# Three edits to a planned instruction order, a product over all 128 rows and a narrower last piece

## The chip, the cores and the metric

The kernel runs on one core of one Trainium2 chip. The metric is the device time in microseconds (us); lower is better.

## The reference, cut to what matters

A linear attention with decay (retention) is followed by a layer normalisation, a feed-forward block and a residual sum.

```python
# q, k, v: 4 x 8 x 768 x 64 float32
for t in range(S):
    state = gamma * state + einsum('bhd,bhe->bhde', k[:, :, t], v[:, :, t])
    y[:, :, t] = scale * einsum('bhd,bhde->bhe', q[:, :, t], state)
x = y.transpose(0, 2, 1, 3).reshape(4, 768, 512)
xn = (x - mean(x)) / sqrt(var(x) + 1e-6) * g_ln
out = x + relu(xn @ w_ch1) @ w_ch2          # 512 -> 2048 -> 512
```

## The kernel before

The 3072 rows are 24 tiles of 128. Tiles 0 to 3 are the first chunks of the four batches and need no state; tiles 4 to 23 are the later chunks. A tile passes through these steps, under the names that the profile shows:

- `tp<-idn,k`, `tp<-idn,qsb`: k and q transposed on TensorE (tiles 0 to 7; from tile 4 on k is called `ksb`).
- `pa<-trq,trk`: the scores. `asb`: the scores times the decay mask, on VectorE ("mask n" below).
- `py<-v,asb`: the masked scores times v ("py n").
- Statistics and `xn` on VectorE; `tp<-idn,xn`: x transposed on TensorE ("x n"); `xnt`: its copy.
- `mm<-xnt,w`: a product of the first layer. 16 matmuls, 0.89 us, are one product of a one-tile group. w1 arrives in four quarters, and product m(n, quarter i) needs the i-th.
- `mm<-zeros`: filler. Until 20 us the planner puts products on zeros into TensorE's planned gaps. They count as busy.
- `tp<-w,h`: a product of the second layer.
- `vg`: v times decay, on GpSimd; `pd<-vg,k`: the state product, which needs it.

The order of the instructions on every engine is decided by a planner inside the program. It puts tasks on engines one at a time, by the earliest *planned* start and then by rank. Durations and load landings are numbers in the code, so a planned number changes the order, and how many fillers there are, and nothing else:

```python
def add(self, eng, ns, rank, emit, after=(), takes=None, uses=(), load=0, lat=0, at=0, follows=()): ...
# ... in order():
            if t["load"]:
                dma_free = max(dma_free, t["end"]) + t["load"]
                t["seen"] = dma_free + self.load_lat + t["lat"]     # planned landing
```

The parts that the change touches:

```python
ones = const.tile([1, P], FP32, name="ones")
grow = const.tile([1, DM], FP32, name="grow")
...
small = a(DVE, 1200, -100, c_small)                    # constants, on VectorE
nc.tensor.matmul(p, lhsT=ones, rhs=grow, ...)          # spreads g over 128 rows
...
loaded[kind, j] = a(POOL, ns, rank, emit, (), takes, uses, dma,
    1500 if kind in "qkv" and j > 7 else 0 if kind in "qkv" else 600, follows=follows)   # "lat"
...
am = a(DVE, 1230, r + 1, e_am, [pat, maskd], ("asb", t), [("pa", t)])      # mask n
xnn = a(DVE, 750, r + 3, e_xn, [bn, gl], ("xn", t), [("py", t)])           # xn n
pdt = a(PE, 230, r - 1 if cc == 0 else r + 2.2, e_pd, [vgt, loaded["k", j]] + ...)
...
for t, cols in [(t, slice(0, DM)) for t in range(NT - 1)] + [              # second layer
        (NT - 1, slice(i * DM // 2, (i + 1) * DM // 2)) for i in range(2)]:
```

## Time and profile before

| what | before |
|---|---|
| time | 217.70 us, median of 3 runs (217.66 to 217.73) |
| the profiled execution | 217.94 us, span 216.2 us, mean clock 0.992 |
| TensorE busy | 207.7 us, 96% |
| VectorE, ScalarE, GpSimd busy | 56%, 39%, 41% |
| first matmul of the last tile | 208.93 us |
| from there to the end of the span | 7.24 us |

Read this by stages, not by the 96%. The profiled execution is 0.24 us above the median, and it is the one that all traces below are compared with. TensorE takes its instructions in order, so a wait costs most where work that is ready stands behind it: in this trace py 3 was ready with its mask at 22.68 and ran at 24.03, behind the wait for `ksb`.

### The profile page before, as it was taken

What the parts mean: (1) busy time and instruction counts of PE and PEld (TensorE: products, weight loads), DVE (VectorE), ACT (ScalarE), POOL (GpSimd) and SP (SyncE); (2) the same over time, 40 slices, a digit from 0 to 9 for tenths busy, and PEclk for the clock granted to TensorE, in tenths of its full rate; (3) what the DMA queues carried; (4) which work ended last, traced back from release to release, by engine and by line L of the source; (5) the groups of instructions that cost most, each with busy time, mean ns of one, the idle gap of its engine ahead of it and who ended that gap; (6) DMA issues with size and microseconds to landing.
All of it is one profiled execution on the core that took longest, in us unless ns stands there. A gap on an engine that the chain in (4) does not pass through costs nothing.

```text
span 216.2 us, 4571 instructions
## 1 busy us (share of the span) xinstructions
PE 207.7 (96%) x1887; PEld 131.8 (61%) x1906; DVE 120.1 (56%) x229; ACT 84.9 (39%) x157; POOL 89.6 (41%) x105
## 2 busy tenths in 40 slices
PE   7898799999999999999999999999999999999993
PEld 7687799996656577566657544554544444444452
DVE  6686677991127987999899855861511100111121
ACT  5456466865222325333316533563442334332000
POOL 8997697969953269863596100000000000000000
PEclk9889999999999999999999999999999999999999
DMA  7999999999999999999999993111121001110212
GB/s 143 178 180 179 180 156 196 206 162 146 134 183 184 176 208 132 142 184 167 193 149 172 127 229 87 50 24 36 40 73 49 13 36 52 49 49 0 100 51 95
DMA packets 106694, 26.51 MB, mean 123 GB/s; under 512 B 99377, under 2 KB 103729, under 8 KB 106674
## 3 DMA queue, kind: packets, MB, share of 16 engines
q0 software_dynamic: 75984, 13.24, 82.0%
q1 hardware_dynamic: 29506, 12.59, 30.1%
q10 hardware_dynamic: 1184, 0.39, 0.7%
q8 instruction: 15, 0.25, 0.4%
q14 instruction: 5, 0.04, 0.1%
HBM read 27.27 MB, written 6.29 MB: 155 GB/s over the span
## 4 chain that ended last, share of the span: by engine, by line
PE 87%; DMA 8%; POOL 2%; issue 1%; DVE 0%; POOLq 0%
PE tp L617 38%; PE mm L580 37%; DMA ksb<-in_k_dram 4%; DMA w<-in_moe_w_ch_dram 3%; PE pa L434 3%; PE py L457 2%; PE pd L503 2%; PE py L453 2%; PE tp L533 1%; PE tp L395 0%; POOL k L337 0%; POOL state L267 0%; PE tp L402 0%; POOL vg L490 0%; POOL qsb L337 0%
## 5 line engine op out<-in xcount | busy, mean ns | idle before, releaser
L580 PE MATMUL mm<-xnt,w 128*128 128x128 bf16 (+2 forms) x768 | 93.7, 273 | 0.5 <-ACT xnt L184 0.5
L617 PE MATMUL tp<-w,h 128*128 128x512 bf16 (+1 forms) x381 | 86.5, 370 | 1.2 <-issue 0.3
L593 ACT ACTIVATE h<-mm 128x512 bf16<-128x512 f32 x91 | 54.4, 598 | 78.8 <-PE mm L580 78.7
L580 PEld LDWEIGHTS <-w 128*128 128x128 bf16 x768 | 58.3, 98 | 24.7 <-issue 0.5
L617 PEld LDWEIGHTS <-h 128*128 128x128 bf16 x400 | 38.0, 98 | 38.4
L625 DVE SCALAR_TENSOR_TENSOR osb<-tp,rstd,x_all 128x512 f32<-128x512 f32 (+1 forms) x25 | 18.2, 728 | 69.0 <-PE tp L617 68.9
L441 DVE TENSOR_TENSOR asb<-pa,mask 128x1024 bf16<-128x1024 f32 x24 | 29.3, 1219 | 7.3 <-PE pa L434 7.0
L471 DVE BATCH_NORM_STATS2 bns<-py 128x6 f32<-128x512 f32 x24 | 16.7, 697 | 10.7 <-PE py L457 10.2
L490 POOL TENSOR_TENSOR vg<-vsb,vsc 128x512 bf16<-128x512 bf16 x16 | 17.2, 1076 | 10.1 <-DMA vsb<-in_v_dram 4.8
L477 ACT CAST x_all<-py 128x512 bf16<-128x512 f32 x24 | 14.0, 582 | 16.7 <-DVE xn L466 15.6
L337 POOL DMA_DIRECT2D vsb<-in_v_dram x20 | 18.1, 909 | 2.1 <-PE py L457 2.1
L337 POOL DMA_DIRECT2D qk<-in_k_dram x16 | 14.7, 920 | 10.1 <-DMA tr<-qk 8.1
L466 DVE SCALAR_TENSOR_TENSOR xn<-py,mv,gb 128x512 bf16<-128x512 f32 x24 | 18.0, 751 | 0.9
L517 DVE TENSOR_TENSOR state<-pd,gch 64x256 bf16<-64x256 f32 x40 | 16.7, 418 | 0.8 <-PE pd L503 0.5
L337 POOL DMA_DIRECT2D qk<-in_q_dram x16 | 14.3, 894 | 2.0 <-DMA w<-in_moe_w_ch_dram 1.4
L641 PE MATMUL mm<-zeros 128*128 128x128 bf16 x84 | 9.3, 277 | 1.0 <-DVE zeros L217 1.0
L424 DVE TENSOR_TENSOR trq<-tr,qsc 128x512 bf16<-128x512 bf16 x16 | 8.4, 527 | 0.2
L641 PEld LDWEIGHTS <-zeros 128*128 128x128 bf16 x84 | 7.5, 129 | 1.3 <-DVE zeros L217 1.0
L457 PEld LDWEIGHTS <-asb 128*128 128x128 bf16 x192 | 8.1, 99 | 0.1
L457 PE MATMUL py<-vsb,asb 128*128 128x64 bf16 x160 | 7.9, 193 | 0.0
L453 PE MATMUL py<-state,trq 128*128 128x128 bf16 x80 | 7.7, 219 | 0.0
L453 PEld LDWEIGHTS <-trq 128*128 128x128 bf16 x80 | 5.8, 98 | 2.3
(64 smaller groups left out, 116.2 us busy)
## 6 DMA issues: line engine op xcount, KB each, us to landing
out_dram<-osb SPq DMA_DIRECT2D x23, 256.0 KB, 2.0
w<-in_moe_w_ch_dram POOLq DMA_DIRECT2D x8, 512.0 KB, 9.7
vsb<-in_v_dram POOLq DMA_DIRECT2D x20, 128.0 KB, 8.8
qk<-in_k_dram POOLq DMA_DIRECT2D x16, 128.0 KB, 8.4
qk<-in_q_dram POOLq DMA_DIRECT2D x16, 128.0 KB, 8.6
qsb<-in_q_dram POOLq DMA_DIRECT2D x7, 128.0 KB, 7.8
ksb<-in_k_dram POOLq DMA_DIRECT2D x4, 128.0 KB, 9.1
k<-in_k_dram POOLq DMA_DIRECT2D x3, 128.0 KB, 7.1
```

The source lines that it names most:

```text
L337: nc.gpsimd.dma_start(out=tile_of(kind, j), in_=src)
L441: nc.vector.tensor_tensor(out=take("asb", t, [P, NPAIR, 2, P], BF16).rearrange("p i a t -> p a i t"), in0=held["pa", t], in1=mask.rearrang ...
L453: nc.tensor.matmul(py[:, 2 * i:2 * i + 2, :], lhsT=held["trq", t][:, i, :], rhs=held["pb", t][:, i, :], start=(mi == 0), stop=False)
L457: nc.tensor.matmul(py[:, h, :], lhsT=held["asb", t][:, h // 2, h % 2, :], rhs=tile_of("v", t)[:, h, :], start=(mi == 0), stop=(mi == n - 1))
L466: nc.vector.scalar_tensor_tensor(out=take("xn", t, [P, DM], BF16), in0=held["py", t].rearrange("p h d -> p (h d)"), scalar=mv[:, t, 0:1], ...
L471: nc.vector.bn_stats(out=bns[:, t, :], in_=held["py", t].rearrange("p h d -> p (h d)"))
L490: e.tensor_tensor(out=take("vg", j, [P, H, D], BF16), in0=tile_of("v", j), in1=vsc[:, cc, :].unsqueeze(2).to_broadcast([P, H, D]), op=ALU. ...
L580: nc.tensor.matmul(p[:, j, :], lhsT=w1[:, ko, (ho + j) * P:(ho + j + 1) * P], rhs=held["xnt", hb][:, h0:h0 + n, ko, :], start=(ko == 0), s ...
L593: nc.scalar.activation(out=dst, in_=src, func=AF.Relu)
L617: nc.tensor.matmul(held[key], lhsT=held["h1", hb][:, ho, i * P:(i + 1) * P], rhs=w2[:, ho, cols], start=(ho == 0), stop=(ho == HO - 1))
L625: nc.vector.scalar_tensor_tensor(out=take("osb", key, [P, w], FP32), in0=held[key], scalar=rstd[:, t:t + 1], in1=x_all[:, t, cols], op0=AL ...
L641: nc.tensor.matmul(held["mm", "warm"][:, 0:P], lhsT=zeros, rhs=zeros, start=True, stop=True)
```

## The change

Five parts:

1. g is multiplied over all 128 rows (zeros below the first), meant to keep TensorE's clock up; this costs a memset.
2. Mask n of tiles 1 to 3 is planned behind xn of tile n-1.
3. q, k and v of tiles 2 to 7 are *planned* to land 0.8 us later, and those of tile 1 0.6 us later; no load is moved by this alone.
4. The first state product is planned at 20 us or later.
5. The last tile's two column halves become 384 and 128 columns.

```diff
-    ones = const.tile([1, P], FP32, name="ones")
-    grow = const.tile([1, DM], FP32, name="grow")
+    ones = const.tile([P, P], FP32, name="ones")
+    grow = const.tile([P, DM], FP32, name="grow")
...
+        nc.vector.memset(grow, 0.0)
...
-    small = a(DVE, 1200, -100, c_small)
+    small = a(DVE, 1450, -100, c_small)
...      (the load of g now fills row 0 and waits for small)
-   1500 if kind in "qkv" and j > 7 else 0 if kind in "qkv" else 600,
+   1500 if kind in "qkv" and j > 7 else 800 if kind in "qkv" and j > 1 else 600,
...
-        am = a(DVE, 1230, r + 1, e_am, [pat, maskd], ("asb", t), [("pa", t)])
+        am = a(DVE, 1230, r + 1, e_am, [pat, maskd] + ([xnn] if 0 < t < 4 else []), ("asb", t), [("pa", t)])
...
-   [("vg", j), where["k", j]] + ([("pd", b)] if cc else []))
+   [("vg", j), where["k", j]] + ([("pd", b)] if cc else []), at=0 if cc or b else 20000)
...
-            (NT - 1, slice(i * DM // 2, (i + 1) * DM // 2)) for i in range(2)]:
+            (NT - 1, slice(0, DM - P)), (NT - 1, slice(DM - P, DM))]:
```

At the first use of `am` for a tile, `xnn` is still that of the tile before, which is what part 2 uses.

More of the change, by code (lines that the diff above doesn't have):

```diff
@@ L292 @@
     grd = a(SP, 390, -150, lambda eng: nc.sync.dma_start(
-        out=grow, in_=moe_g_ln.rearrange("(o n) -> o n", o=1)), load=10)
+        out=grow[0:1, :], in_=moe_g_ln.rearrange("(o n) -> o n", o=1)), [small], load=10)
     gbm = a(PE, 1000, 2, c_gb, [grd, small2], ("mm", "g"), at=7600)
```

## The prediction

> **What bounds the kernel now.** I began with the busy shares over the span on the page, then cut the span into windows.
>
> ```profile
> PE   7898799999999999999999999999999999999993
> ...
> PEclk9889999999999999999999999999999999999999
> ...
> DMA  7999999999999999999999993111121001110212
> ```
>
> Each digit is a fortieth of the span, 5.4 us. TensorE is full from the fifth or sixth digit to the last but one; before that it is not, and there the DMA engines are full. So there are three stages: a head that lives on loads, a body of pure TensorE work, and a tail after the last matmul.
>
> ```profile
> core 0: us, PE busy (x) PEld busy (x) DVE busy (x) ACT busy (x) POOL busy (x), PEclk, DMA share, GB/s
> ...
> 9.40:12.80 3.40, 3.40 (x42) 3.00 (x40) 2.69 (x6) 1.42 (x7) 2.97 (x5) 0.53 1.99 171
> ...
> 20.00:24.30 4.30, 2.59 (x47) 2.06 (x45) 2.19 (x3) 2.17 (x5) 2.24 (x4) 1.00 1.95 176
> 24.30:212.40 188.10, 186.78 (x1610) 114.12 (x1625) 103.00 (x182) 72.62 (x132) 69.80 (x76) 1.00 1.09 118
> 212.40:216.20 3.80, 0.19 (x2) 0.00 (x0) 0.48 (x1) 0.00 (x0) 0.00 (x0) 1.00 0.18 61
> ```
>
> In the body, 24.3 to 212.4, PE is busy 186.8 of 188.1 us. The few steps there between two 512-column matmuls that are 0.43 us and not 0.22 are lost records, not waits: the group of the second product has 381 records of the 400 that its weight loads count. So the time is: end of the body = (real matmul work, which the change leaves alone) + (TensorE time in the head that did no real work), then a tail of 3.8 us. The change can gain only by doing more real work before about 24 us, or by shortening the tail. The window 20.0 to 24.3 is the worst: 1.7 us of 4.3 are empty. Who is waited for there:
>
> ```profile
> PE tp L395 <- DMA ksb<-in_k_dram: 0.8, 1, 0.8
> PE mm L580 <- ACT xnt L184: 0.5, 1, 0.5
> PE tp L395 <- DMA k<-in_k_dram: 0.5, 1, 0.5
> PE tp L533 <- DVE xn L466: 0.4, 1, 0.4
> ```
>
> The timeline puts three of the four there, and the k load at 7.5:
>
> ```profile
> 16.71 1.95 PE L580 MATMUL mm<-xnt,w 128*128 128x128 bf16 x32
> ...
> 18.50 0.40 PE L457 MATMUL py<-v,asb 128*128 128x64 bf16 x8
> ...
> 20.69 0.40 PE L533 MATMUL tp<-idn,xn 128*128 128x128 bf16 x4 [0.38 <-DVE xn L466]
> ...
> 21.96 1.05 PE L580 MATMUL mm<-xnt,w 128*128 128x128 bf16 x16 [0.55 <-ACT xnt L184]
> ...
> 23.80 0.40 PE L395 MATMUL tp<-idn,ksb 128*128 128x128 bf16 x4 [0.78 <-DMA ksb<-in_k_dram]
> ```
>
> TensorE runs in order. The transpose of tile 4's k, at 23.80, waits for a load that lands at 23.75, while tile 3's py (mask ready at 22.68) and a 16-matmul product of w1's third quarter (landed 22.39) stand behind it. That is the wait to remove.
>
> **What the Trainium skill says.** "TensorE: Matmul & The Clock Gate", Part 1, says the clock halves or doubles by windows of 3413 ns. The trace agrees: the granted clock is 0.5 for one 3.41 us record, 9.21 to 12.62, and matmuls step by 107 ns there against 56 before and after. The page gives idleness as the cause; here PE was busy 2.95 of the 3.5 us before, but 0.5 us of it was the one-row product for g. Whether one row counts as idle the page does not say; the change bets on it. Its rules section says a product over few rows takes the time of one over 128, so all rows should cost nothing against today's 1.12 us. "VectorE: DVE Perf Modes", on zero memsets, gives one cycle per element whatever the type; 128 f32 took 0.17 us and one took 0.06 here, so the new 512-wide memset is, as an estimate, 0.06 + 511 x 0.11/127 = 0.5 us. "DMA: Bandwidth & Descriptors", Anatomy, gives about 2.0 us fixed per DMA; the stores here land in 2.0 us at 256 KB and 1.7 at 128 KB, so a smaller last store saves little.
>
> **The change part by part.** I compared the built order of both kernels, engine by engine.
>
> *Memset of 128x512 on VectorE, all rows of ones:* +0.5 us in the constants. VectorE ends them at 4.77 and is then idle 0.47 until q lands (5.24): at most 0.1 us late, and see below for why that is lost anyway. The small load of g now waits for the memset (about 0.5 us later); its product starts near 8 us.
>
> *Masking of tiles 1 to 3 behind the x of the tile ahead:* VectorE's order of these is already mask, statistics, x, mask. The new edge pins it. 0.
>
> *Tile 0's scores before tile 1's k transpose:* takes it from behind the k wait. Scores 0 started at 7.79 though trq was ready at 7.31: 0.35 us sooner.
>
> *g over 128 rows:* if the clock stays full, the chain from 9.2 to 12.5 (q1 transpose, py0, scores 1, x0 transpose, each 0.53 to 0.63 instead of 0.40) is about 0.3 to 0.7 us sooner.
>
> *First state product put off:* the state update, two instructions of 0.42 us, leaves its place between trq2 (ends 15.89) and mask 2 (starts 16.68): mask 2 about 0.45 us sooner.
>
> These could make tile 2 more than 1 us earlier, but all of that meets one load: w1's second quarter, issued at 7.51, lands at 17.31, and py2 stands behind its product. It starts at 17.60 now, so at most 0.25 us of it survives: py2 at 18.25.
>
> *Loads of tiles 2 to 7 planned later:* this is the part that pays. From py2, with durations of the trace (16 matmuls 0.89, a transpose set 0.22, py 0.23, scores 0.33): k3 18.5, product 18.7 to 19.6, q3 and first state product to 20.1, x2 transpose 20.45 (0.24 sooner), scores 3 at 20.8. State update now comes before mask 3: mask 3 ends 22.75, as before. Then two products in place of one, 21.7 to 23.5, py3 to 23.75, k4 as it lands (23.8 to 24.0), product to 24.9, q4, product to 26.05, x3 transpose. It was at 27.17 with the same work done: 1.1 us ahead.
>
> *What is given back:* the order of GpSimd's queue changes too. Tile 7's k load is now issued ahead of tile 4's vg. GpSimd comes free at 26.03; issue 0.94, then vg 1.06: vg4 ends at 28.0 instead of 27.11. Its product stands right behind scores 4, which TensorE now reaches at 27.2 and leaves at 27.5: a new wait of 0.5 us. From 28.05 the lead is about 0.6 us. A little slack upstream changes nothing, as vg4 hangs on issues and landings alone.
>
> *Behind that:* VectorE has no idle time from 36.75 to 49.7, with slack of 0.2 us at tile 7's scores. The new order answers: one 0.69 us relu of that stretch goes to ScalarE and one product moves ahead of tile 7's scores. I keep the 0.6. The later loads have 4 us and more to spare from landing to use, and the last groups have the old order.
>
> *Tail:*
>
> ```profile
> 210.94 0.48 DVE L625 SCALAR_TENSOR_TENSOR osb<-tp,rstd,x_all 128x256 f32<-128x256 f32 x1 [1.05 <-PE tp L617]
> 212.63 0.48 DVE L625 SCALAR_TENSOR_TENSOR osb<-tp,rstd,x_all 128x256 f32<-128x256 f32 x1 [1.21 <-PE tp L617]
> 213.15 0.36 ACTq L632 DMA_DIRECT2D out_dram<-osb  x1
> ```
>
> The halves of 256 become 384 and 128 columns. Matmuls: 32 x 0.109 = 3.49 us before; 16 x 0.163 (between 0.109 and 0.216) + 16 x 0.056 = 3.50 after. The last VectorE step: 512 columns take 0.75 and 256 take 0.48, so 128 take 0.35: -0.13. The last store has 64 KB for 128: about -0.1 by the slope above, less if the larger store, now issued only 0.6 us ahead, is in its way. -0.15 in all.
>
> Sum: -0.6 - 0.15 = -0.75, from 217.7 to 216.95; I say 216.9.
>
> **The rivals.** (a) *The loads bind, and nothing moves:* DMA is 90% full and more until 130 us, and the change moves no byte. For it: w1's landings at 17.3 and 22.4. Against it: between those TensorE has real work ready and stands still for order alone. Then only the tail is left: 217.5. (b) *vg4 does not hold:* the v4 data are there at 24.9; if GpSimd's issues come sooner, the whole 1.1 us and the tail come through: 216.4. (c) *VectorE takes over at 37 to 49 us:* a lead cannot pass an engine without idle time. For it: no gap there. Against: the moved relu, and products that need no VectorE to fill in. It would leave 0 to 0.3: 217.3. (d) *The clock:* if the half-speed record moves to 12.6 to 16.0, where real products begin, 16 matmuls cost 1.7 and not 0.9 us: py1 and x1 late, up to +0.5 after the meeting point at 17.3: 217.5.
>
> **Range and chances.** The terms run from -0.15 to -1.3, the middle near -0.75; I widen for landings that shift by some tenths: 216.2 to 217.5. Two per cent is 4.4 us, more than all empty TensorE time of the head after 12 us, so within 2% is all but sure.
>
> **What would show it.** Right: PE's wait for ksb at tile 4's k near 0; the x3 transpose near 26.05; a new wait of PE's state product for vg of some 0.5 us near 27.5; no granted clock of 0.5 at 9.2 to 12.6, with py2 still near 18.25; the dense body ending at about 211.8; the last VectorE step 0.35. Wrong: w1's second quarter landing elsewhere than 17.3, PE waits for VectorE between 37 and 50, or new gaps of PE in the body.

## The result, and the profile after

| | runs, us | median |
|---|---|---|
| before, in the same rounds | 217.66 to 217.82 | 217.71 |
| changed | 217.65, 216.83, 216.84, 216.83 | 216.84 |

The ratio is 0.9968, with a 95% interval of 0.9945 to 0.9992. A ratio here is the mean time of one kernel's runs over that of the other's of the same rounds, so it is not quite the ratio of the medians. The medians differ by 0.87 us: faster. The three shorter runs have spans of 215.0 us; **the profiled execution is the slowest of the four**, 217.65 with a span of 215.8, which matters below.

The busy shares in forty slices, after:

```profile
PE   7888899999999999999999999999999999999993
PEclk9999999999999999999999999999999999999999
DMA  7999999999999999999999993111121011110212
```

The second and third digits of the clock were 8 and are 9: no half-speed record in the head. (One begins at 214.86, after the last matmul.) The rest has the old shape, so the gain has to be sought in single waits. The same windows as before:

```profile
core 0: us, PE busy (x) PEld busy (x) DVE busy (x) ACT busy (x) POOL busy (x), PEclk, DMA share, GB/s
...
9.40:12.80 3.40, 2.73 (x49) 2.20 (x46) 3.07 (x5) 1.60 (x5) 2.89 (x5) 1.00 1.97 173
20.00:24.30 4.30, 2.82 (x47) 2.32 (x45) 2.62 (x5) 2.00 (x4) 1.96 (x3) 1.00 1.96 177
24.30:212.40 188.10, 186.76 (x1606) 113.24 (x1620) 103.44 (x181) 73.90 (x133) 69.90 (x77) 1.00 1.07 118
212.40:216.20 3.80, 0.04 (x1) 0.00 (x0) 0.35 (x1) 0.00 (x0) 0.00 (x0) 0.82 0.21 69
```

In 9.4 to 12.8 the clock is 1.00 and not 0.53. In 20.0 to 24.3, where the gain was to come from, TensorE is busy 2.82 us and not 2.59: little. Who it waits for:

```profile
PE mm L581 <- DMA w<-in_moe_w_ch_dram: 0.9, 1, 0.9
...
PE tp L534 <- DVE xn L467: 0.6, 1, 0.6
PE mm L581 <- ACT xnt L184: 0.4, 1, 0.4
```

The wait for `ksb`, 0.8 us before, is gone, as planned, but one for a quarter of w1 stands in its place. The timeline places it:

```profile
16.19 2.16 PE L581 MATMUL mm<-xnt,w 128*128 128x128 bf16 x32 
18.18 0.40 PE L458 MATMUL py<-v,asb 128*128 128x64 bf16 x8 
...
20.38 0.40 PE L534 MATMUL tp<-idn,xn 128*128 128x128 bf16 x4 [0.23 <-ACT h L594]
...
21.48 1.05 PE L581 MATMUL mm<-xnt,w 128*128 128x128 bf16 x16 [0.38 <-ACT xnt L184]
23.41 1.07 PE L581 MATMUL mm<-xnt,w 128*128 128x128 bf16 x16 [0.88 <-DMA w<-in_moe_w_ch_dram]
...
24.54 0.39 PE L396 MATMUL tp<-idn,ksb 128*128 128x128 bf16 x4 
```

The second of the two products that now stand ahead of tile 4's k needs w1's third quarter. It landed at 22.39 before and at 23.36 here. The tail:

```profile
211.64 0.62 DVE L626 SCALAR_TENSOR_TENSOR osb<-tp,rstd,x_all 128x384 f32<-128x384 f32 x1 [1.90 <-PE tp L618]
212.48 0.35 DVE L626 SCALAR_TENSOR_TENSOR osb<-tp,rstd,x_all 128x128 f32<-128x128 f32 x1 [0.22 <-PE tp L618]
212.86 0.36 ACTq L633 DMA_DIRECT2D out_dram<-osb  x1
```

The last VectorE step is 0.35 and not 0.48 us. From the last tile's first matmul (208.78) to the end of the span it is 7.04 us, before 7.24. So in this execution the head gave 208.93 - 208.78 = 0.15 and the tail 0.20. In the three shorter runs, if their tail is the same, the last tile starts at 215.0 - 7.04 = 207.96, about 0.8 us earlier than here. What differs between executions of one program is the first question for the experiments.

### The profile page after: what moved, and what is told of

It is laid out like the page before. It is cut to its first block, busy times and chain, and to the rows that moved or that the text cites. A ratio compares the mean times of both kernels' runs of the same rounds, so it can differ in the third digit from the quotient of the medians.

```text
span 215.8 us, 4578 instructions
## 1 busy us (share of the span) xinstructions
PE 206.9 (96%) x1892; PEld 130.7 (61%) x1910; DVE 120.3 (56%) x229; ACT 86.2 (40%) x158; POOL 89.7 (42%) x105
## 4 chain that ended last, share of the span: by engine, by line
PE 86%; DMA 9%; POOL 1%; DVE 1%; issue 1%; POOLq 0%
PE tp L618 38%; PE mm L581 37%; DMA w<-in_moe_w_ch_dram 9%; PE pa L435 3%; PE pd L504 2%; PE py L458 2%; PE py L454 2%; DVE asb L442 1%; PE tp L534 1%; DVE trq L425 0%; POOL k L338 0%; PE tp L403 0%; PE tp L396 0%; POOL qsb L338 0%; POOL v L338 0%
## 5 line engine op out<-in xcount | busy, mean ns | idle before, releaser
L618 PE MATMUL tp<-w,h 128*128 128x512 bf16 (+2 forms) x382 | 86.4, 370 | 1.1 <-issue 0.2
L594 ACT ACTIVATE h<-mm 128x512 bf16<-128x512 f32 x92 | 55.0, 598 | 75.9 <-PE mm L581 75.6
L618 PEld LDWEIGHTS <-h 128*128 128x128 bf16 x400 | 37.4, 98 | 39.1
L626 DVE SCALAR_TENSOR_TENSOR osb<-tp,rstd,x_all 128x512 f32<-128x512 f32 (+2 forms) x25 | 18.2, 729 | 68.3 <-PE tp L618 68.2
L425 DVE TENSOR_TENSOR trq<-tr,qsc 128x512 bf16<-128x512 bf16 x16 | 9.5, 591 | 0.3
L642 PE MATMUL mm<-zeros 128*128 128x128 bf16 x88 | 8.6, 260 | 1.0 <-DVE zeros L217 1.0
```

The lines of the kernel that those rows point to most:

```text
L594: nc.scalar.activation(out=dst, in_=src, func=AF.Relu)
L618: nc.tensor.matmul(held[key], lhsT=held["h1", hb][:, ho, i * P:(i + 1) * P], rhs=w2[:, ho, cols], start=(ho == 0), stop=(ho == HO - 1))
L626: nc.vector.scalar_tensor_tensor(out=take("osb", key, [P, w], FP32), in0=held[key], scalar=rstd[:, t:t + 1], in1=x_all[:, t, cols], op0=AL ...
```

## The experiments

**My theory:** the planned landings make the gain in the head, and it depends on w1's third quarter landing by 22.4; the split makes the tail; parts 1, 2 and 4 are worth nothing. **The rivals:** the late quarter is a lasting effect of the new order; the clock makes the gain; the other edges matter.

All twelve kernels were correct, with five rounds each. The first four ran on one chip, beside 11 runs of before with a median of 217.71; the other eight on a second chip, beside 11 or 12 with a median of 217.92 or 217.89. I compare kernels within a chip. "w1 third" is that quarter's landing in the profiled execution.

| kernel | median (range), us | ratio [95%] | w1 third |
|---|---|---|---|
| *first chip* | | | |
| changed kernel again | 217.0 (216.75 to 217.27) | 0.9964 [0.9951, 0.9977] | 23.16 |
| without the later landings | 217.53 (217.43 to 218.23) | 0.9997 [0.9985, 1.0009] | 22.18 |
| g over one row | 217.06 (216.71 to 219.51) | 0.9987 [0.9954, 1.0019] | 22.42 |
| tile 7's k held back (missed) | 216.98 (216.63 to 218.12) | 0.9971 [0.9953, 0.9989] | 22.15 |
| *second chip* | | | |
| tile 7's k behind vg 4 | 217.06 (216.9 to 217.24) | 0.9958 [0.9941, 0.9975] | 22.30 |
| w1 third planned later | 216.92 (216.81 to 217.17) | 0.9955 [0.9935, 0.9974] | 22.48 |
| both of these | **216.72** (216.59 to 217.47) | 0.9947 [0.9928, 0.9965] | 22.20 |
| last tile in halves | 217.22 (217.2 to 217.28) | 0.9965 [0.9948, 0.9981] | 22.21 |
| without the mask edge | 217.98 (217.44 to 218.48) | 0.9998 [0.9977, 1.0019] | 22.44 |
| state product not put off | 216.94 (216.85 to 217.22) | 0.9953 [0.9937, 0.9969] | 22.34 |
| before + later landings only | 217.48 (217.01 to 217.92) | 0.9978 [0.9958, 0.9997] | 22.20 |
| four loads planned as seen | 217.37 (217.17 to 217.51) | 0.9971 [0.9955, 0.9986] | 22.33 |

### The changed kernel again

No edit.

> The changed kernel unaltered, for more of its times and a second trace. The profiled execution of it took 217.65 us and not 216.83 like the other three, and in its trace w1's third quarter landed at 23.36 where the kernel before had it at 22.39; the product of tile 0 with it waited 0.9 us. Theory: two kinds of execution, by that landing. A trace of a 216.8 us execution has the landing near 22.4, PE's wait for w near 0, and a wait of some 0.5 us of tile 4's state product for vg near 27.5. Rival: the landing is always near 23.4 and the short executions gain elsewhere; then the trace of a short one still shows the 0.9 us wait.

The gain repeats (0.71 us between the medians; whether this is another chip than that of the first result is not on record), and so does the late quarter: 23.16, with a wait for it.

```profile
PE mm L581 <- DMA w<-in_moe_w_ch_dram: 1.0, 1, 1.0
```

So it is not a single accident. But it is not in every execution either. The kernels below that have the same order up to that point saw it at 22.1 to 22.5, as the kernel before did. In 14 traces it was late twice, both times in the unaltered changed kernel, and the load is issued at the same place in the queue in all of them. Two of two against none of twelve might look like the changed kernel's own. Against that, three of its four first runs were 0.8 us faster than the one that was profiled; and the kernel with the halves at the end, whose head has the same order, saw 22.21. What moves the landing by 1 us is not shown. The traces do hold a lead. A load's semaphore counts sixteen steps. In the 12 early traces fifteen steps of the third quarter are in by 21.28 to 21.62 and the last comes at 22.15 to 22.48; in the two late ones the fifteenth comes at 22.32 and 22.01, the sixteenth at 23.36 and 23.16. In all 14 traces one 16 KB transfer of queue q8, which the profile calls "instruction", runs for 0.89 to 0.95 us from about 14; then the second quarter's fifteenth step is in by 16.20 to 16.55 and its sixteenth 0.6 to 1.2 us later. So the landing near 17.3 at which everything meets is itself one straggler of sixteen. A second such transfer starts at 20.9 to 21.7 (22.5 without the mask edge), while the third quarter arrives. This suggests that a fetch of instructions holds up one of the load's steps; but the packets don't name the DMA engine, so it is likely and not shown.

How much does the late quarter cost? The kernel with the halves has the same head and the early quarter. Against it the profiled changed execution is 0.88 us behind at 26.5, but only 0.32 from 29.65 on, since it has no wait for vg 4; a wait of 0.18 for VectorE's `trq` at 67.93, which two kernels with an early quarter also have, makes most of the rest of the 0.63 at the last tile (208.78 against 208.15). So the late quarter costs some 0.3 us, and not all of the 0.8 between the first result's runs. Where the rest lies stays open.

### Without the later landings

```diff
-   800 if kind in "qkv" and j > 1 else 600
+   0 if kind in "qkv" else 600
```

> The changed kernel with the planned landing of tiles 2 to 7 put back to the old value. In the built order k4's transpose is again ahead of py3 and of tile 0's product with w1's third quarter, and tile 7's k load is again behind tile 4's vg; the rest of the change stays. Theory (the later loads are the part that pays, 0.6 us): 217.4 to 217.6, with a wait of some 0.8 us for ksb at 23.8. Rival (loads bind anyway; clock, masks and tail make the gain): 216.8 to 216.9.

The old wait comes back:

```profile
PE tp L396 <- DMA ksb<-in_k_dram: 0.7, 1, 0.7
```

The medians leave 217.71 - 217.53 = 0.18 us of gain, which is the tail's 0.20. (The means, with one run of 218.23 among these, leave 0.07.) The edit takes back tile 1's 0.6 too: running the planner, without the chip, shows that tile 1's number alone only puts tile 0's scores ahead of tile 1's k transpose, and tiles 2 to 7 make the rest of the new order. This part carries the head's gain.

### g over one row

```diff
-    ones = const.tile([P, P], FP32, name="ones")
+    ones = const.tile([1, P], FP32, name="ones")      # grow likewise; no memset, no edge from small
```

> The changed kernel with g's product over one row again and no memset of 128x512; every engine's order else is the same. Theory (all of the head meets at the landing of w1's second quarter at 17.3): time within 0.1 us of the changed kernel, 216.8, with or without a half-speed record at 9 to 13 us. Rival (the clock makes the gain): 217.2 or more, with a granted clock of 0.5 in the windows 9.4 to 12.8.

The bet on rows is not borne out: with one row the clock in the windows 5.9 to 9.4 and 9.4 to 12.8 was 1.00 as well. The ratio is blurred by one run of 219.51, of unknown cause; two of its six runs were 216.84, as was the changed kernel's first median. Each run also lists its mean granted clock over the span. One half-speed record of 3.41 us lowers that by 3.41 x 0.5 / 216 = 0.8%, to 0.992. Among the 11 runs of before on this chip, three lie at 0.991 or 0.992: 217.96, 217.58 and 217.68, with a mean of 217.74. The mean of the other eight is 217.76. **So here the record that the change set out to remove cost no time that could be told**, as the prediction argued: everything before 17.3 meets at w1's second quarter. That is not so of every slow record. On the second chip the two runs of before whose clock of 0.982 and 0.983 stands for about two records are its slowest, 218.57 and 218.58; and the one run of "tile 7's k held back" with a record (0.990) is that kernel's slowest, 218.12. The mean clock doesn't tell where in a run a record lay, so what one costs elsewhere, or in the new order, is open.

Are such records rarer with 128 rows? Over all runs, a mean clock of 0.993 or less was seen in 9 of the 30 with the head of before (24 of its runs whose clock is listed, and six of "before + later landings"), in 1 of 59 of the changed kernel and its variants with 128 rows, and in none of the six with one row in the new order. They are rarer, but whether by the rows or by the order is open: at 9 in 30, six runs without one come up one time in eight (0.7 to the sixth power).

### Tile 7's k load behind tile 4's vg, in two tries

In the changed kernel, GpSimd issues tile 7's k load ahead of vg 4, which then ends at 28.2 and not at 27.1:

```profile
26.24 0.90 POOL L338 DMA_DIRECT2D ksb<-in_k_dram  x1
27.13 1.08 POOL L491 TENSOR_TENSOR vg<-vsb,vsc 128x512 bf16<-128x512 bf16 x1
```

The first try held this load back alone:

```diff
+   at=25300 if (kind, j) == ("k", 7) else 0
```

> The changed kernel with tile 7's k load issued behind tile 4's vg, as in the kernel before; no other instruction moves. Theory (the prediction's give-back): vg4 ends at 27.1, the wait of tile 4's state product is gone, and short executions take 216.3 to 216.4. Rival (TensorE reaches that product late for another reason): 216.8 as the changed kernel, and the long executions, if there are any, stay at 217.6.

It was misdesigned: tile 7's q load slipped into the freed place, vg 4 still ended at 27.96, and TensorE waited 0.38 us for it; the lowest run, 216.63, misses the expected 216.3 to 216.4. The second try moved the queue behind it too, so that in GpSimd's queue only k 7 and vg 4 change places:

```diff
+   at=25100 if j > 6 and kind in "qkv" or kind == "w2" else 0
```

> What i_vg was meant to be: tile 4's vg directly behind tile 6's v load in GpSimd's queue, tile 7's k load behind it; no other instruction moves on any engine (in i_vg tile 7's q load had slipped into the place of its k load). Theory (the give-back of the prediction is real, but the loads that follow are a further bound: in the traces of u_g and i_vg, where w1's third quarter came early, TensorE waited 0.3 to 0.4 us for vg4 and was then again no further at tile 5's py than where it had come late): vg4 ends near 27.0, its wait is gone, and the median is 216.6 to 216.9. Prediction's rival b taken whole: 216.3 to 216.4.

Now vg 4 runs from 25.99 to 27.05 and TensorE's wait for it is gone. A smaller one stands further down, at 34.95, where v 6 landed at 33.69:

```profile
PE pd L505 <- POOL vg L492: 0.3, 1, 0.3
```

Taken alone it changes no time that could be told (0.9958, against 0.9953 for a variant with the old queue on the same chip), and its 217.06 lies above the expected 216.6 to 216.9.

### w1's third quarter planned where it may land

```diff
-   800 if kind in "qkv" and j > 1 else 600
+   800 if kind in "qkv" and j > 1 else 1600 if (kind, j) == ("w1", 2) else 600
```

> The changed kernel with w1's third quarter planned to land 1 us later: on TensorE the product of tile 2 with w1's second quarter, whose inputs are all there, goes ahead of tile 0's with the third; three products change places, one relu each on VectorE and ScalarE, nothing else. Theory (in the executions where that quarter lands at 23.2 and not 22.2 the changed kernel waits 0.9 us for it): no wait for w in PE's list, x3's transpose near 26.0 whichever it is, then the wait for vg4 of 0.3 to 0.5; the median 216.8 and a narrower spread than the changed kernel's 216.75 to 217.65. Rival (the landing only marks slow executions, which are slow elsewhere too): spread and median as before, 217.0.

Three products change places, so that a product with the second quarter is ahead of the one that needs the third. In the execution that was profiled the quarter landed early (22.48), so the trace can't show a wait avoided; vg 4 was waited for, 0.38 us, and the second quarter at 17.44, 0.47. The five runs span 0.36 us, against 0.82 and 0.52 for the changed kernel's two sets. That would suit a kernel that no longer depends on the landing, but the kernel with the last tile in halves, which has the changed kernel's head, spans 0.08, so it shows nothing. The median is 216.92.

### Both edits together

> Both of the above together. Theory: with neither the third quarter nor vg4 in the way TensorE keeps its lead of 1.1 us up to tile 6's k, which lands near 31.0 to 31.8 and is then waited for some 0.3 us: 216.3 to 216.6, the fastest so far. Rival (the total of loads binds at every later point): 216.8.

From 20 us on TensorE waits for neither w nor vg. The two longest waits left there:

```profile
PE mm L582 <- ACT xnt L184: 0.4, 1, 0.4
PE tp L397 <- DMA ksb<-in_k_dram: 0.4, 1, 0.4
```

Its median of 216.72 is the lowest of all, though above the expected 216.3 to 216.6: 1.2 us under the kernel before of the same rounds, and in median under the changed kernel (216.84 and 217.0 in its two sets, not run beside it). It beats before clearly. Against the changed kernel the intervals of the ratios overlap (0.9928 to 0.9965, and 0.9951 to 0.9977), so that lead is likely and not shown.

### The last tile in halves again

```diff
-            (NT - 1, slice(0, DM - P)), (NT - 1, slice(DM - P, DM))]:
+            (NT - 1, slice(i * DM // 2, (i + 1) * DM // 2)) for i in range(2)]:
```

> The changed kernel with the last tile in two halves of 256 columns again; nothing else moves. Theory: +0.15 us against the changed kernel of the same chip and rounds (the last VectorE step 0.48 instead of 0.35, the last store 128 KB instead of 64), so 217.1 to 217.2 beside 217.0. Rival (the larger first store holds up the second): within 0.05 of the changed kernel or faster.

From the last tile's first matmul to the end it is 7.23 us, against 7.04 in both traces of the changed kernel: the tail is worth 0.2. This execution also shows the changed kernel's head with the early quarter, the case that I had predicted:

```profile
23.78 0.40 PE L396 MATMUL tp<-idn,ksb 128*128 128x128 bf16 x4 [0.22 <-DMA ksb<-in_k_dram]
...
26.03 0.39 PE L534 MATMUL tp<-idn,xn 128*128 128x128 bf16 x4 
...
28.01 0.38 PE L504 MATMUL pd<-vg,ksb 128*128 128x128 bf16 x4 [0.38 <-POOL vg L491]
```

The transpose of x 3 is at 26.03, before 27.17, with four products between x 2 and x 3 in both. Then 0.38 is given back to vg. Its last tile starts at 208.15, which is 0.8 before the profiled 208.93 of the kernel before.

### Without the mask edge

```diff
-   [pat, maskd] + ([xnn] if 0 < t < 4 else [])
+   [pat, maskd]
```

> The changed kernel without the edge that puts the masks of tiles 1 to 3 behind the x of the tile ahead. The prediction called this part nothing, because VectorE's order in the kernel before is that one already. But with the rest of the change the planner now puts mask 1 ahead of x0, so the x0 transpose, the first product and all of tile 0's and 1's x come 1.2 us later on VectorE; TensorE's order of products changes with it. Theory (the head meets at the load of w1's second quarter, at 17.1 to 17.4, and the first product has 3 us to spare before it): x0's transpose near 12.9 instead of 11.7, and the time within 0.3 us of the changed kernel, 216.8 to 217.3. Rival (the edge is what protects the head): the gain is gone, 217.5 or more.

**My expectation was wrong and the rival right: the gain is gone** (0.9998). Against "state product not put off" on the same chip the edge is worth (0.9998 - 0.9953) x 217.9 = 1.0 us. The order explains it. With the other parts in place, the plan could start the first tile's `xn` at 10630 ns, because the copy of g ends then, and mask 1 at 10620: ten planned nanoseconds put the mask first. The first tile's x comes later, and the planner answers by putting tile 0's product with w1's second quarter ahead of tile 1's with the first. TensorE then stands before that landing:

```profile
17.40 1.96 PE L581 MATMUL mm<-xnt,w 128*128 128x128 bf16 x32 [0.81 <-DMA w<-in_moe_w_ch_dram]
19.20 0.40 PE L458 MATMUL py<-v,asb 128*128 128x64 bf16 x8 
```

py 2 is at 19.20 and not at 18.18. Later the wait for vg 4 is 0.6 us, and tiles 4 to 7 come through their x transposes 1.6 to 4.2 us later than in the changed kernel.

That microsecond holds beside the other parts only. Running the planner without the chip shows that where g is taken over one row, leaving the edge out changes no instruction's place; nor does it without the later landings. So it is part 1, with its memset, together with the later landings that would flip the order, and the edge takes the flip back. No run leaves both out.

### The state product not put off

```diff
-   at=0 if cc or b else 20000
```

> The changed kernel with the first state product where it was, behind the first product of the feed-forward part; only it and its state update move. Theory: mask 2 starts 0.4 us later but py2 stands behind the product with w1's second quarter in any case (it had 1.05 us of slack in the trace of the changed kernel), and mask 3 no longer has the state update ahead of it: time within 0.15 us of the changed kernel, py2 near 18.2. Rival (putting it off makes part of the gain): 217.1 to 217.3.

As expected: 216.94, and py 2 at 18.20. What the put-off product frees on VectorE goes to a mask that has slack: in the changed kernel mask 2 is ready 1.05 us before py 2.

### The kernel before with the later landings alone

```diff
-   0 if kind in "qkv" else 600          # in before
+   800 if kind in "qkv" and j > 1 else 600
```

> The kernel before with the planned landing of tiles 2 to 7 alone. Theory (this is the part that pays, and it needs no other): 0.5 to 0.7 us faster than the kernel before, with the old tail: 217.0 to 217.3, and no wait for ksb at tile 4's k. Rival (it pays only together with the other edges): 217.6 or more.

The median gains 0.4 us, somewhat less than I expected, and the runs are spread over 0.9. In the profiled one (217.19) the wait for `ksb` is 0.2 and that for vg 0.4. So this part works alone too, without the mask edge: by the planner its order is that of "state product not put off", but for the last tile's pieces.

### Four loads planned as they had been seen to land

```diff
+   late = {("w1", 2): 1600, ("k", 4): 1200, ("k", 6): 1700}   # in the place of 600 or 800; and the at=25100 from above
```

> The changed kernel with w1's third quarter planned 1 us later, tile 4's k 0.4 later, tile 6's k 0.9 later, and tile 7's k load behind tile 4's vg. On TensorE tile 0's product with the third quarter now stands between py3 and tile 4's k, and tile 6's k transpose behind scores 5; further down some products change places. Theory (what is left of TensorE's waits after 22 us are single loads, and each can be put behind work that is ready): no wait of PE from 22 to 36 us, and 216.3 to 216.6. Rival (the order further down costs as much, or the sum of the loads binds): 216.7 or more, with new waits of PE between 30 and 50 us.

TensorE indeed has no wait from 22 to 36 us, and the time is worse by 0.65 than with two of the edits. The later order changed with it:

```profile
51.85 1.02 PE L619 MATMUL tp<-w,h 128*128 128x512 bf16 x4 [0.72 <-DVE osb L627]
```

A second-layer product waits for its accumulator, which VectorE frees by the sum for tile 0. That sum is queued behind tile 7's steps, whose x transpose is now at 50.74 and was at 49.13 with two of the edits. Another wait, of 0.21, is at 127 us. The rival was right in the main, though it had looked for the wait at 30 to 50 us: a plan that suits the head better shifted a wait further down.

## Why the prediction was right or wrong

The time was right: 216.84 measured, 216.9 predicted. Term by term:

- **Tail, -0.15 predicted, -0.20 measured** (7.24 to 7.04, and 7.23 with the halves back). The mechanism holds: the last VectorE step is 0.35, as read off the three sizes. The last store, 1.67 us from issue to landing and 1.74 before, saved little.
- **Head, -0.6 predicted.** The first medians differ by 0.87 and the second by 0.71; less the tail, that is 0.67 and 0.51. The steps hold: in the execution with the changed kernel's head and an early third quarter, py 2 is at 18.08 for 18.25 predicted, x 3 at 26.03 for 26.05.
- **What is given back, 0.5 predicted, 0.38 measured**, from 27.63 to 28.01 for 27.5 to 28.0: right mechanism, somewhat smaller. It is absent when the quarter is late, since TensorE then gets there after vg.
- **The step that was missed:** "a 16-matmul product of w1's third quarter (landed 22.39)" was taken as fixed. I put that product ahead of k 4 without asking what happens when the quarter is late. It was late by 1 us in both traces of the changed kernel, and then x 3 is at 26.78 or 26.57 and the head's lead at the last tile is 0.15 or 0.5 (208.78 and 208.41 against 208.93 in an execution of before that was itself 0.24 above the median). The quarter alone costs some 0.3 of that, as told above; the wait for `trq` in one of the two was not foreseen either. My "landings that shift by some tenths" was too small for this load, though the range held.
- **Masking edge, "0": wrong for the edge by itself.** VectorE's order in the kernel before was already the wanted one, and I took that as the edge's worth. But part 1 and the later landings together move the plan, and without the edge they would flip this order and lose about 1 us. As I compared the built orders of the whole kernels, 0 was right for the two together, and so the total came out right; that the one is needed against the other I hadn't seen.
- **The clock:** predicted full, and it was; worth nothing that could be told, as predicted, because of the landing at 17.3. That the 128 rows do it is not shown. The working misread one figure: of the 2.95 us that TensorE was busy there, the one-row product made 1.12 (8.11 to 9.23) and not 0.5, and fillers 0.77 more. Over 128 rows the product took 1.08, so the rows were free, as said. The memset took 0.48 us, for an estimated 0.5. Scores 0 were to come 0.35 sooner and came 0.11 sooner (7.79 to 7.68). VectorE had cast q at 6.09 in both, but its cast of v, which stands ahead of `trq` in its queue, waited for v until 6.87 and not 6.55; that gain too had nowhere to go.
- **First state product:** its 0.45 us was said to be lost at the same landing, and undoing it alone moved no time.
- **Rivals:** (a) did not come; "without the later landings" reaches its number, 217.53, but by the order and not by moved loads. (b) did not come: vg 4 held. (c) did not come to the changed kernel, but a wait of that kind, for VectorE near 50 us, accounts for the loss in the last experiment (0.72 for 0.65). (d) was not seen in a trace; the slow-clock runs above may be such cases.
- **The end of the dense body,** predicted at 211.8: the last matmul ended at 212.59 before, at 212.44 in the late execution, and at 211.81 in the early one with the same head.

## What to carry to other kernels

In a stage that lives on loads, an in-order engine gains by what stands *behind* a landing, so put ready work ahead of the load that is waited for, and check which landing that work itself hangs on and how far it varies between executions. In a planned schedule a part has no worth of its own: judge an edge by undoing it inside the whole change, and again together with the part that it answers, since ten planned nanoseconds can flip an order that costs a microsecond. Before removing a visible blemish, such as one slow clock record, look whether everything after it meets at a later landing anyway. When a load lands late in some executions, look at its single steps: here fifteen of sixteen were in 1 us before the last.

## What the Trainium skill lacked or had wrong

- "TensorE: Matmul & The Clock Gate", Part 1, gives an idle window as what halves the clock. It doesn't say how busy a window must be to count as idle. In the kernel before TensorE was busy 2.95 of the 3.5 us before the half-speed record, of which the one-row product made 1.12 and fillers on zeros 0.77; in the one-row variant, with 2.84 of 3.5, the clock stayed at 1.00. The records come and go between runs of one program (3 of 11 on one chip).
- The same page, in its terms, gives the cost of a slow stretch as the slow time times one minus the granted share. For 3.41 us at half speed that is, as an estimate, 1.7 us; here runs of one kernel with such a record have a mean of 217.74 us and those without 217.76. The page doesn't say that the cost is an upper bound where a stage waits for loads.
- "DMA: Bandwidth & Descriptors", Latency and other measured facts, says that latency to memory grows from 0.2 to 2 us under load. It has no figure for how far one load's landing moves between executions of the same program: here 22.15 to 23.36 us for a w1 quarter, with the DMA engines full. Whether that latency is the cause no run shows. No page gives a figure for what a 16 KB "instruction" transfer costs a load beside it; here such a transfer, of 0.89 to 0.95 us, goes with a last step that comes 0.6 to 1.2 us after the fifteenth.
- The same page, Anatomy, gives 2.0 us fixed per DMA, for those that GpSimd issues. It has no such figure for stores that other engines issue: here they took 1.67 us at 64 KB, 1.70 to 1.75 at 128 KB and 2.0 at 256 KB from issue to landing.
- No page tells how a load's issue on GpSimd delays compute on the same engine. It is 0.9 us an issue, and one such issue moved vg 4 from 27.1 to 28.2.
